# Attention with a soft mixture of experts behind it: the first query block's maxima as an F32 product, and one tile for two heads' last scores

## The chip, the cores and the metric

The kernel runs on one core of a Trainium2 chip. The metric is device time in microseconds (us). Six names recur: PE is TensorE (matmul), PEld its weight loads, DVE is VectorE, ACT is ScalarE, POOL is GpSimd, SP issues the DMAs. PSUM is the memory into which PE writes; SBUF is the main on-chip memory.

## The reference

Eight batches of eight heads attend over 576 tokens of 64 channels, with a decay and a causal mask; then 4608 tokens of 512 channels go through a soft mixture of eight experts with four slots each.

```
scores = q @ k.T / 8 + cum[:, None] - cum[None, :]      # cum = cumsum(log(clip(f)))
scores = where(causal, -1e9, scores); scores -= max(scores, -1)
attn = exp(scores) / (sum(exp(scores)) + 1e-9); x = attn @ v
logits = x @ phi
slots = softmax(logits over tokens).T @ x               # then per expert: relu(s @ w1) @ w2
out = softmax(logits over slots) @ slot_out
```

## The kernel before

Heads are taken in 32 pairs, one pair per turn of the main loop (`for g in range(1, NG)`, L695), four pairs to a batch. `w = (g - 4) % 4` tells which of a batch's side jobs a turn carries: logits at w 0, their maximum and weights at w 1, combine weights and dispatch at w 2 and 3. The order of every engine's work is the order of the calls in the program; an engine takes its instructions in that order, and semaphores make one wait for another. All DMAs are issued by SP in one queue.

For a head there are two passes over the scores. The first finds each query's maximum: `s1` (L215) multiplies a block of 128 queries by the keys that come before it, into one of three PSUM buffers `s`, and `tops` (L230) adds the mask and takes the maximum on DVE (L239: a custom operation and an accumulator read that writes a column of `MT`). `TOPS` lists six such pieces: number 2 is block 4 against keys 0 to 287, where the mask is zero throughout; number 5 is block 0, 64 queries padded to 128 against 64 keys. `mturn` (L244) turns `MT` of a pair on PE, `mrows` copies the rows on ACT, and a DMA puts them into the operand `YA`, so that the second pass gets scores with the maximum already taken off.

The second pass, `s2` (L263), multiplies keys by queries into a ring of three PSUM tiles, as two matmuls for high and low parts (L276, L277). `SEGS` lists the pieces; the last tile of a head holds 256, 192 and 64 columns for key chunks 0, 3 and 4 (piece 5 is chunk 4, 64 keys by 64 queries). `expo` (L283) takes the exponential on ACT into `PTS`, which holds two heads; `causal` (L285) zeroes the triangles on POOL in three operations (L291 for chunks 0 to 2 in one, L294 for chunk 3 and for chunk 4). `s3` (L303) multiplies by the values into `pv[0]` (first head) or `pv[1]` (second head), 25 products a head in the order `VALUES` (L69, L70): products of 64 queries alternate between the lower and the upper 64 partitions of the output (u = 0 and u = 1), 13 of the one kind and 12 of the other. Each F32 product is two matmul instructions. `norm` (L318) divides on DVE.

A turn works on different pairs at once. It does `s2` and `s3` of pair g (heads h0, h1), and `s1` and `tops` of heads u0 = h0 + 3 and u1 = h0 + 4, so that u0 completes the maxima of pair g + 1. The turn starts with `s2(h0, 0)` and `norm` of the head before; `tops(u0)` follows; `mturn(g + 1)` stands after `s2(h1, 2)`; `s3(h0)` and `s3(h1)` end the turn. On DVE `mgroup` (w 1) and `combine(b, 0)` (w 2) stand between `norm` and `tops(u0, 2)`. `px` (L352) turns results of pair g - 1 on PE into free columns of the `pv` tiles, and `xcopy` copies them on ACT; `px(g - 1, 4)` uses columns 325 to 452 of `pv[1]`.

Of the kernel before, what the change touches and what calls it, by code (L numbers as in the profile page):

```python
# [7 lines left out]
F32 = mybir.dt.float32  # L8
# [13 lines left out]
NBLK = 5  # L22
# [45 lines left out]

HALF = [[(t, u, c) for t in (4, 3, 2, 1, 0) if t < 4 or u == 0 for c in range(queries(t, u) // 2 + 1)] for u in range(2)]  # L69
VALUES = [x for n in range(13) for h in HALF for x in h[n : n + 1]]  # L70

@with_exitstack
def attn_softmoe(ctx: ExitStack, tc: tile.TileContext, qk, v, f, phi, w1, w2, cst, out):
# [156 lines left out]
    def tops(i, *which):  # L230
        if not head(i):
            return
        g, h = divmod(i, 2)
        for n in which:
            bank, o, blk, j0, w = TOPS[n]
            t = st["top", i % 2, bank]
            m0 = max(448 - (128 * blk + 64) + j0, 0)
            top = MT[g % 3][:, NBLK * h + blk : NBLK * h + blk + 1] if g else m2[h][:, blk, 1:2]
            nc.vector.tensor_tensor_reduce(  # L239
                out=t[:, o : o + w], in0=t[:, o : o + w], in1=mask[:, m0 : m0 + w], scale=1.0, scalar=top if n == 3 else -3.0e38,  # L240
                op0=ALU.add, op1=ALU.max, accum_out=top,
            )
# [19 lines left out]

    def s2(i, *which):  # L263
        if not head(i):
# [3 lines left out]
        for n in which:  # L268
            bank, c, i0, w = SEGS[n]
            t, at = (turn(), 0) if n < 4 else st["bank"]  # L270

            n = 128 if c < 4 else 64
            o = t[0:n, at : at + w]
            at += w
            j0 = S * h + 128 * c
            nc.tensor.matmul(o, wa[0:m, j0 : j0 + n], ya[0:m, h, 64 + i0 : 64 + i0 + w], start=True, stop=False)  # L276
            nc.tensor.matmul(o, wb[:, j0 : j0 + n], yb[:, h, i0 : i0 + w], start=False, stop=True)  # L277
            st["bank"] = t, at

# [4 lines left out]

    def causal(i):  # L285

# [4 lines left out]
        nc.gpsimd.affine_select(d3, d3, pattern=[[0, 3], [1, 128]], compare_op=ALU.is_ge, fill=0.0, base=0, channel_multiplier=-1)  # L291
        for o, w in ((pt_col(3, 384), 128), (pt_col(4, 512), 64)):
            dd = pt[:, o : o + w]
            nc.gpsimd.affine_select(dd, dd, pattern=[[1, w]], compare_op=ALU.is_ge, fill=0.0, base=0, channel_multiplier=-1)  # L294

    def blank(t):
# [6 lines left out]
    def s3(i, n0=None, n1=None):  # L303
# [4 lines left out]
        for t, u, c in VALUES[n0:n1]:  # L308
# [3 lines left out]
                o[64 * u : 64 * u + 64, t, :], PT[i % 2][:, at : at + 64], V[:, g % 2, c, 65 * h : 65 * h + 65], start=(c == 0), stop=(c == r // 2)  # L312
            )

    def xtile(b, u):
# [188 lines left out]
    load_qk(1)  # L504
    nc.vector.memset(fin, 1.0)
    nc.scalar.activation(fin[:, 0:1], fin[:, 0:1], AF.Ln)
    nc.vector.memset(fy, 1.0)
# [69 lines left out]
    def first(i, n, busy=0):  # L577
        s1(i, *GROUPS[n])
        warm(busy, cs)
        tops(i, *GROUPS[n])  # L580

# [34 lines left out]
    first(2, 3)  # L616
    causal(0)
    low_k(2)
# [19 lines left out]
    low_k(3)  # L638
    causal(1)
    low_q(3)  # L640
# [54 lines left out]
    for g in range(1, NG):  # L695
# [11 lines left out]
        expo(h0, 0)  # L707
        norm(h0 - 1)
        if w == 1:
            mgroup(b)  # L710
# [7 lines left out]
        tops(u0, 3)  # L718
        if g > 1:
            px(g - 1, 0)  # L720
        s2(h0, 2)
        expo(h0, 2)
        if g > 1:
            px(g - 1, 3)
        else:
            round_k(3, 0)
            round_q(3, 0)
# [9 lines left out]
        s2(h0, 4)  # L737
        s1(u0, 4, 5)
        s2(h0, 5)
        expo(h0, 3)  # L740
        tops(u0, 4, 5)
        causal(h0)
# [25 lines left out]
        s2(h1, 3, 4)  # L768
        s1(u1, 4, 5)
        s2(h1, 5)  # L770
        expo(h1, 3)
        tops(u1, 4, 5)
        causal(h1)
# [308 lines left out]
```

## Time and profile before

| | us |
|---|---|
| median of 3 runs | 400.83 (400.12 to 402.21) |
| the profiled execution | 401.76 |
| its span, first to last instruction | 400.1 |
| PE busy | 380.7 (95%) |
| weight loads busy | 333.1 (83%) |
| DVE busy | 282.9 (71%) |
| ACT busy | 262.5 (66%) |
| POOL busy | 250.8 (63%) |

A row of a timeline gives start and duration in us, engine, line, operation, output and inputs, shapes and count; what stands in brackets is the idle time before it and what ended it. Rows of the same kind that follow each other are merged. A weight load has a row of its own (PEld). A matmul's duration contains its way through the array, so the distance from one start to the next is what it costs. Operations of DVE can overlap in the rows: the next starts before the one before has ended. The mean granted clock of TensorE was 0.983.

### The profile page before, as it was taken

Reading aid. Unit: us, or ns where it says so; the run is one execution under the profiler, and the core shown is the slowest. Engines: PE = TensorE matmul, PEld = TensorE weight load, DVE = VectorE, ACT = ScalarE, POOL = GpSimd, SP = SyncE. Lnnn points to the kernel's source line nnn. Section 1 sums busy time; section 2 is a strip of 40 time slices with the busy share of each in tenths; the row PEclk is TensorE's granted clock in tenths of the full one; section 3 lists DMA queues with packets and bytes.
Section 4 is the critical chain, followed back from the end, with each engine's and each line's share of the span. In section 5 each row is a group of like instructions: output and inputs, shape, how many; then the busy total and the mean of one; then the engine's idle time right before and its main releaser. Section 6 shows DMA issues by size and latency. Waiting matters only on the chain.

```text
span 400.1 us, 15146 instructions
## 1 busy us (share of the span) xinstructions
PE 380.7 (95%) x5843; PEld 333.1 (83%) x5843; DVE 282.9 (71%) x1130; ACT 262.5 (66%) x675; POOL 250.8 (63%) x341
## 2 busy tenths in 40 slices
PE   8999999999999999999999999999999998999880
PEld 7889999999989999999999989999999885444540
DVE  7878887879767978787888778877878444312571
ACT  8859777767776777668777786777776542240450
POOL 4697887878767877787878777877787520000000
PEclk9999999999999999999999999999999999999985
DMA  6866767777777777777777677877675699999798
GB/s 206 209 159 161 231 169 207 205 210 209 206 208 207 209 207 208 210 208 207 209 208 225 201 209 204 225 209 214 199 185 151 240 343 350 409 407 387 247 378 333
DMA packets 34744, 93.72 MB, mean 234 GB/s; under 512 B 4282, under 2 KB 9072, under 8 KB 34672
## 3 DMA queue, kind: packets, MB, share of 16 engines
q1 hardware_dynamic: 34672, 92.75, 75.1%
q8 instruction: 46, 0.75, 0.8%
q14 instruction: 26, 0.21, 0.2%
HBM read 63.93 MB, written 9.73 MB: 184 GB/s over the span
## 4 chain that ended last, share of the span: by engine, by line
PE 90%; DMA 3%; ACT 2%; DVE 1%; issue 1%; SPq 0%; DVEq 0%; ACTq 0%
PE pv L311 25%; PE ring L276 13%; PE s L226 12%; PE ring L277 12%; PE pv L338 4%; PE pv L936 4%; PE more L899 4%; PE lg L374 3%; PE ring L491 3%; PE ring L1016 2%; PE ds L455 2%; DMA RAW<-in_qk 2%; DMA out<-RAW 1%; PE ring L684 1%; PE pv L249 1%; ACT PTS L283 1%
## 5 line engine op out<-in xcount | busy, mean ns | idle before, releaser
L283 ACT ACTIVATE PTS<-ring 128x320 f32<-128x320 f32 (+2 forms) x256 | 119.5, 513 | 61.3 <-PE ring L277 33.8
L239 DVE CUSTOM_DVE_ANT_0 s<-s,mask 128x320 f32<-128x320 f32 (+4 forms) x320 | 137.4, 449 | 5.3 <-PE s L226 0.8
L276 PE MATMUL ring<-YA,WA 67*128 67x320 f32 (+9 forms) x384 | 121.8, 330 | 0.0
L277 PE MATMUL ring<-YB,WB 128*128 128x320 f32 (+4 forms) x384 | 110.7, 296 | 0.0
L311 PE MATMUL pv<-V,PTS 128*64 128x65 f32 x3200 | 104.3, 223 | 0.7 <-ACT mr L258 0.7
L311 PEld LDWEIGHTS pv<-V,PTS 128*64 128x64 f32 x3200 | 99.6, 137 | 3.4 <-ACT mr L258 1.2
L226 PE MATMUL s<-WA,YA 66*128 66x288 f32 (+9 forms) x384 | 98.6, 312 | 1.7 <-ACT PTS L283 1.3
L205 POOL TENSOR_TENSOR WB<-RAW,WB 64x576 fp32r<-64x576 f32 x64 | 90.3, 1410 | 11.0 <-DMA WB<-WA 5.0
L210 POOL TENSOR_TENSOR YB<-RAW,YA 64x576 fp32r<-64x576 f32 x64 | 89.3, 1414 | 2.5
L276 PEld LDWEIGHTS ring<-YA,WA 67*128 67x128 f32 (+3 forms) x384 | 69.7, 183 | 5.4 <-issue 2.1
L277 PEld LDWEIGHTS ring<-YB,WB 128*128 128x128 f32 (+1 forms) x384 | 69.9, 182 | 0.0
L226 PEld LDWEIGHTS s<-WA,YA 66*128 66x128 f32 (+1 forms) x384 | 63.0, 190 | 7.8 <-ACT PTS L283 2.4
L294 POOL TENSOR_SCALAR_AFFINE_SELECT PTS<-PTS 128x128 f32<-128x128 f32 (+1 forms) x128 | 31.3, 265 | 35.2 <-ACT PTS L283 32.3
L239 DVE DVE_READ_ACCUMULATOR2_ANT MT<- 128x1 f32 x372 | 52.5, 141 | 0.0
L291 POOL TENSOR_SCALAR_AFFINE_SELECT PTS<-PTS 128x384 f32<-128x384 f32 x64 | 33.3, 520 | 25.8 <-ACT PTS L283 22.8
L179 ACT CAST WA<-RAW 64x576 fp32r<-64x576 f32 x64 | 40.1, 669 | 12.8 <-DMA RAW<-in_qk 12.3
L338 PE MATMUL pv<-cs,X 128*128 128x128 f32 x155 | 42.1, 277 | 0.2 <-DVE lg L805 0.2
L239 DVE CUSTOM_DVE_ANT_0 s<-s,mask,MT 128x288 f32<-128x288 f32 x62 | 32.6, 526 | 11.2 <-PE s L226 2.2
L184 ACT CAST YA<-RAW 64x576 fp32r<-64x576 f32 x63 | 39.4, 669 | 0.4
L326 DVE TENSOR_SCALAR rl<-pv 128x5 f32<-128x5 f32 x64 | 10.5, 164 | 33.2 <-PE pv L311 32.7
L331 DVE TENSOR_TENSOR X<-pv,rl 128x320 f32<-128x320 f32 (+1 forms) x65 | 31.5, 486 | 2.4 <-DMA YA<-mr 0.3
L362 ACT COPY XT<-pv 128x128 f32<-128x128 f32 (+1 forms) x124 | 28.6, 292 | 0.0
(184 smaller groups left out, 353.5 us busy)
## 6 DMA issues: line engine op xcount, KB each, us to landing
w<-in_w SPq DMA_DIRECT2D x46, 512.0 KB
RAW<-in_qk SPq DMA_DIRECT2D x31, 576.0 KB
V<-in_v SPq DMA_DIRECT2D x32, 325.0 KB
YB<-YA SPq DMA_DIRECT2D x30, 288.0 KB
WB<-WA SPq DMA_DIRECT2D x30, 288.0 KB
p<-in_w SPq DMA_DIRECT2D x7, 512.0 KB
out<-p SPq DMA_DIRECT2D x6, 512.0 KB
out<-RAW SPq DMA_DIRECT2D x9, 256.0 KB
```

Of the source, the lines that this page charges most:

```text
L179: nc.scalar.copy(WA[g % 3][0:64, S * h : S * h + S], RAW[g % 3][64:128, h])
L184: nc.scalar.copy(YA[g % 3][0:64, h, 64:640], RAW[g % 3][0:64, h])
L205: nc.gpsimd.tensor_tensor(t[0:64], RAW[g % 3][64:128, h], t[64:128].bitcast(F32), op=ALU.subtract)
L210: nc.gpsimd.tensor_tensor(YB[g % 2][64:128, h], RAW[g % 3][0:64, h], YA[g % 3][0:64, h, 64:640].bitcast(F32), op=ALU.subtract)
L226: nc.tensor.matmul(t[:, o : o + w], ya[0:m, h, 128 * blk : 128 * blk + 128], wa[0:m, j0 : j0 + w], start=True, stop=True)
L239: nc.vector.tensor_tensor_reduce(out=t[:, o : o + w], in0=t[:, o : o + w], in1=mask[:, m0 : m0 + w], scale=1.0, scalar=top if n == 3 else ...
L276: nc.tensor.matmul(o, wa[0:m, j0 : j0 + n], ya[0:m, h, 64 + i0 : 64 + i0 + w], start=True, stop=False)
L277: nc.tensor.matmul(o, wb[:, j0 : j0 + n], yb[:, h, i0 : i0 + w], start=False, stop=True)
L283: nc.scalar.activation(PT[i % 2][:, SEG_O[bank] : SEG_O[bank] + at], t[:, 0:at], AF.Exp, scale=0.125)
L291: nc.gpsimd.affine_select(d3, d3, pattern=[[0, 3], [1, 128]], compare_op=ALU.is_ge, fill=0.0, base=0, channel_multiplier=-1)
L311: nc.tensor.matmul(o[64 * u : 64 * u + 64, t, :], PT[i % 2][:, at : at + 64], V[:, g % 2, c, 65 * h : 65 * h + 65], start=(c == 0), stop=( ...
L338: nc.tensor.transpose(pm[:, 0:128], x[:, t, 128 * (p % 2) : 128 * (p % 2) + 128], ident)
```

## The change

The maxima of block 0 are no longer a piece of `s1` and `tops` in the main loop. Behind the values of a head, at the end of `s3`, stands an F32 product of 64 queries by 64 keys of the head four later, which writes the upper 64 partitions of `pv[1]` in columns 384 to 447 or 448 to 511. `edges`, after `norm` of the next turn, adds the triangle of the mask for both heads in one DVE operation and takes both maxima in a second one, on partitions 64 to 127, into `MT`. Heads 0 to 4 keep the old way. Piece 2 is taken with a plain reduction, without the mask, in all heads.

Chunk 4 of the second pass leaves the last tile of both heads. `corners` computes it for both heads into a ring tile of its own, after `expo(h1, 3)`, with one exponential and one POOL operation for the two, which stands before `causal(h1)`. `causal` in the loop has two operations then. Query block 4, which alone reads chunk 4, moves from the head of `VALUES` to its end. `px(g - 1, 0)` moves behind `s2(h0, 2)`. Three small memsets of `MT` on POOL are added at the start.

```diff
@@ -66,7 +66,7 @@
-HALF = [[(t, u, c) for t in (4, 3, 2, 1, 0) if t < 4 or u == 0 for c in range(queries(t, u) // 2 + 1)] for u in range(2)]
+HALF = [[(t, u, c) for t in (3, 2, 1, 0, 4) if t < 4 or u == 0 for c in range(queries(t, u) // 2 + 1)] for u in range(2)]
 VALUES = [x for n in range(13) for h in HALF for x in h[n : n + 1]]
 @with_exitstack
@@ -236,6 +236,9 @@
             t = st["top", i % 2, bank]
             m0 = max(448 - (128 * blk + 64) + j0, 0)
             top = MT[g % 3][:, NBLK * h + blk : NBLK * h + blk + 1] if g else m2[h][:, blk, 1:2]
+            if n == 2:
+                nc.vector.tensor_reduce(top, t[:, o : o + w], axis=AX.X, op=ALU.max)
+                continue
             nc.vector.tensor_tensor_reduce(
                 out=t[:, o : o + w], in0=t[:, o : o + w], in1=mask[:, m0 : m0 + w], scale=1.0, scalar=top if n == 3 else -3.0e38,
                 op0=ALU.add, op1=ALU.max, accum_out=top,
@@ -260,14 +263,17 @@
         dst = YA[g % 3][m : m + 1, h0:h1].rearrange("c h s -> c (h s)")
         nc.sync.dma_start(dst.bitcast(F32), mr[0:n].bitcast(F32))
-    def s2(i, *which):
+    def s2(i, *which, corner=None):
         if not head(i):
             return
         g, h = divmod(i, 2)
         ya, wa, yb, wb, m = YA[g % 3], WA[g % 3], YB[g % 2], WB[g % 2], TOP[g % 3] + 1
         for n in which:
             bank, c, i0, w = SEGS[n]
-            t, at = (turn(), 0) if n < 4 else st["bank"]
+            if corner is None:
+                t, at = (turn(), 0) if n < 4 else st["bank"]
+            else:
+                t, at = corner, 64 * h
             n = 128 if c < 4 else 64
             o = t[0:n, at : at + w]
@@ -275,23 +281,36 @@
             j0 = S * h + 128 * c
             nc.tensor.matmul(o, wa[0:m, j0 : j0 + n], ya[0:m, h, 64 + i0 : 64 + i0 + w], start=True, stop=False)
             nc.tensor.matmul(o, wb[:, j0 : j0 + n], yb[:, h, i0 : i0 + w], start=False, stop=True)
-            st["bank"] = t, at
+            if corner is None:
+                st["bank"] = t, at
     def expo(i, bank):
         if head(i):
             t, at = st["bank"]
             nc.scalar.activation(PT[i % 2][:, SEG_O[bank] : SEG_O[bank] + at], t[:, 0:at], AF.Exp, scale=0.125)
-    def causal(i):
+    def corners(g):
+
+        t = turn()
+        for h in range(2):
+            s2(2 * g + h, 5, corner=t)
+        o = pt_col(4, 512)
+        to = PTS[:, 0:3200].rearrange("p (h c) -> p h c", h=2)[0:64, :, o : o + 64]
+        nc.scalar.activation(to, t[0:64, 0:128].rearrange("p (h c) -> p h c", h=2), AF.Exp, scale=0.125)
+        nc.gpsimd.affine_select(to, to, pattern=[[0, 2], [1, 64]], compare_op=ALU.is_ge, fill=0.0, base=0, channel_multiplier=-1)
+
+    def causal(i, *more):
         if not head(i):
             return
         pt = PT[i % 2]
         d3 = pt[:, 0:960].rearrange("p (a b) -> p a b", b=320)[:, :, 0:128]
         nc.gpsimd.affine_select(d3, d3, pattern=[[0, 3], [1, 128]], compare_op=ALU.is_ge, fill=0.0, base=0, channel_multiplier=-1)
-        for o, w in ((pt_col(3, 384), 128), (pt_col(4, 512), 64)):
+        for o, w in ((pt_col(3, 384), 128), *more):
             dd = pt[:, o : o + w]
             nc.gpsimd.affine_select(dd, dd, pattern=[[1, w]], compare_op=ALU.is_ge, fill=0.0, base=0, channel_multiplier=-1)
+
+    LAST = (pt_col(4, 512), 64)
     def blank(t):
@@ -311,6 +330,19 @@
             nc.tensor.matmul(
                 o[64 * u : 64 * u + 64, t, :], PT[i % 2][:, at : at + 64], V[:, g % 2, c, 65 * h : 65 * h + 65], start=(c == 0), stop=(c == r // 2)
             )
+        if n1 is None and i and head(i + 4):
+
+            ya, wa, m = YA[(g + 2) % 3], WA[(g + 2) % 3], TOP[(g + 2) % 3]
+            nc.tensor.matmul(
+                pv[1][64:128, 384 + 64 * h : 448 + 64 * h], ya[0:m, h, 64:128].bitcast(F32), wa[0:m, S * h : S * h + 64].bitcast(F32), start=True, stop=True
+            )
+
+    def edges(g, h0=0):
+        if pair(g):
+            t = pv[1][64:128, 384:512].rearrange("p (h c) -> p h c", h=2)[:, h0:2]
+            tri = mask[64:128, 384:448].rearrange("p (o c) -> p o c", o=1).broadcast_to([64, 2 - h0, 64])
+            nc.vector.tensor_tensor(t, t, tri, op=ALU.add)
+            nc.vector.tensor_reduce(MT[g % 3][64:128, NBLK * h0 : 2 * NBLK : NBLK], t, axis=AX.X, op=ALU.max)
     def xtile(b, u):
         return X[(2 * b + u) % 3 if (b, u) != (B - 1, 1) else 3]
@@ -503,6 +535,8 @@
     nc.sync.dma_start(cs, cst[:, 0:258])
     load_qk(1)
     nc.vector.memset(fin, 1.0)
+    for t in MT:
+        nc.gpsimd.memset(t, 0.0)
     nc.scalar.activation(fin[:, 0:1], fin[:, 0:1], AF.Ln)
     nc.vector.memset(fy, 1.0)
     for t in ring:
@@ -575,9 +609,10 @@
     GROUPS = ((0, 1), (2,), (3,), (4, 5))
     def first(i, n, busy=0):
-        s1(i, *GROUPS[n])
+        ns = GROUPS[n]
+        s1(i, *ns)
         warm(busy, cs)
-        tops(i, *GROUPS[n])
+        tops(i, *ns)
     def both(i, n):
         s2(i, *((0,), (1,), (2,), (3, 4, 5))[n])
@@ -614,7 +649,7 @@
     load_qk(3)
     first(2, 2)
     first(2, 3)
-    causal(0)
+    causal(0, LAST)
     low_k(2)
     low_q(2)
     both(1, 0)
@@ -636,7 +671,7 @@
     first(3, 3)
     norm(0)
     low_k(3)
-    causal(1)
+    causal(1, LAST)
     low_q(3)
     first(4, 0)
     warm(2, cs)
@@ -706,6 +741,7 @@
         s2(h0, 0)
         expo(h0, 0)
         norm(h0 - 1)
+        edges(g + 1, int(g == 1))
         if w == 1:
             mgroup(b)
         if w == 2:
@@ -716,11 +752,10 @@
         expo(h0, 1)
         s1(u0, 3)
         tops(u0, 3)
-        if g > 1:
-            px(g - 1, 0)
         s2(h0, 2)
         expo(h0, 2)
         if g > 1:
+            px(g - 1, 0)
             px(g - 1, 3)
         else:
             round_k(3, 0)
@@ -735,10 +770,9 @@
             xcopy(g - 1, (3,))
             px(g - 1, 2)
         s2(h0, 4)
-        s1(u0, 4, 5)
-        s2(h0, 5)
+        s1(u0, 4)
         expo(h0, 3)
-        tops(u0, 4, 5)
+        tops(u0, 4)
         causal(h0)
         low_k(h0 + 2)
         if w == 1:
@@ -766,10 +800,10 @@
         s1(u1, 0, 1)
         tops(u1, 0, 1)
         s2(h1, 3, 4)
-        s1(u1, 4, 5)
-        s2(h1, 5)
+        s1(u1, 4)
         expo(h1, 3)
-        tops(u1, 4, 5)
+        corners(g)
+        tops(u1, 4)
         causal(h1)
         low_k(h1 + 2)
         if g == 1:
```

## Rows read from the trace of the kernel before

**Rows 1.** The page's first part (engine, busy us, share, instructions) and the head of its fourth (the chain that ended last, by engine).
```profile
PE 380.7 (95%) x5843; PEld 333.1 (83%) x5843; DVE 282.9 (71%) x1130; ACT 262.5 (66%) x675; POOL 250.8 (63%) x341
...
PE 90%; DMA 3%; ACT 2%; DVE 1%; issue 1%; SPq 0%; DVEq 0%; ACTq 0%
```

**Rows 2.** The waits of PE, longest in total first (us in total, times, longest): the first two.
```profile
PE ring L491 <- DVE ring L510: 1.9, 1, 1.9
PE s L226 <- ACT PTS L283: 1.3, 2, 0.8
```

**Rows 3.** The timeline of PE in a turn with w 3 (g = 19), from 204.7 to the start of the next turn.
```profile
204.72 0.41 PE L226 MATMUL s<-WA,YA 66*128 66x448 f32 x2
204.97 0.22 PE L276 MATMUL ring<-YA,WA 67*64 67x64 f32 x1
205.03 0.22 PE L277 MATMUL ring<-YB,WB 128*64 128x64 f32 x1
205.09 0.45 PE L276 MATMUL ring<-YA,WA 67*128 67x448 f32 x1
205.37 0.37 PE L277 MATMUL ring<-YB,WB 128*128 128x448 f32 x1
205.58 0.27 PE L338 MATMUL pv<-cs,X 128*128 128x128 f32 x1
...
206.57 0.27 PE L249 MATMUL pv<-cs,MT 128*10 128x128 f32 x1
...
207.39 0.42 PE L226 MATMUL s<-WA,YA 97*128 97x448 f32 x2
207.65 0.22 PE L276 MATMUL ring<-YA,WA 67*64 67x64 f32 x1
207.71 0.22 PE L277 MATMUL ring<-YB,WB 128*64 128x64 f32 x1
207.86 3.25 PE L311 MATMUL pv<-V,PTS 128*64 128x65 f32 x100
211.04 0.47 PE L276 MATMUL ring<-YA,WA 67*128 67x448 f32 x1
```

**Rows 4.** The timeline of DVE in the same turn, from the norm of the head before to the last maximum of u0.
```profile
202.27 0.17 DVE L326 TENSOR_SCALAR rl<-pv 128x5 f32<-128x5 f32 x1 [0.53 <-PE pv L311]
...
202.69 0.49 DVE L331 TENSOR_TENSOR X<-pv,rl 128x320 f32<-128x320 f32 x1
203.10 0.46 DVE L239 CUSTOM_DVE_ANT_0 s<-s,mask 128x288 f32<-128x288 f32 x1
203.47 0.14 DVE L239 DVE_READ_ACCUMULATOR2_ANT MT<- 128x1 f32 x1
203.76 0.53 DVE L239 CUSTOM_DVE_ANT_0 s<-s,mask,MT 128x288 f32<-128x288 f32 x1
...
205.72 0.14 DVE L239 DVE_READ_ACCUMULATOR2_ANT MT<- 128x1 f32 x1
205.90 0.23 DVE L239 CUSTOM_DVE_ANT_0 s<-s,mask 128x64 f32<-128x64 f32 x1
206.05 0.14 DVE L239 DVE_READ_ACCUMULATOR2_ANT MT<- 128x1 f32 x1
```

**Rows 5.** The timeline of all engines in the turn before (w 2, g = 18), where the last maximum of u0 and the turning of `MT` meet.
```profile
196.26 0.14 DVE L239 DVE_READ_ACCUMULATOR2_ANT MT<- 128x1 f32 x1
...
196.46 0.09 PEld L249 LDWEIGHTS pv<-cs,MT 128*10 128x10 f32 x1 [0.17 <-DVE MT L239]
196.46 0.28 PE L249 MATMUL pv<-cs,MT 128*10 128x128 f32 x1
```

**Rows 6.** Groups of DVE instructions by line and form (count, busy us, mean ns, idle before).
```profile
L483 DVE TENSOR_REDUCE ring<-ring 128x5 f32<-128x160 f32 x8 | 2.6, 327 | 4.4 <-ACT ring L479 4.4
L486 DVE TENSOR_TENSOR ctok<-ring,sm 128x160 f32<-128x160 f32 x8 | 2.6, 325 | 0.3
L389 DVE TENSOR_REDUCE mb<-LG 128x1 f32<-128x193 f32 x7 | 2.5, 355 | 6.8 <-ACT LG L381 6.8
L475 DVE TENSOR_REDUCE sm<-tk 128x5 f32<-128x160 f32 x7 | 2.3, 326 | 3.2 <-ACT LD L444 3.2
L239 DVE CUSTOM_DVE_ANT_0 s<-s,mask 128x64 f32<-128x64 f32 x64 | 14.9, 232 | 2.2
```

**Rows 7.** The timeline of DVE at the start of the program: memsets of all partitions (L526), then of partitions 64 to 127 (L299, L300).
```profile
4.45 0.08 DVE L526 MEMSET LG<- 128x10 f32 x2
4.54 0.11 DVE L299 MEMSET pv<- 64x64 f32 x1
4.73 0.06 DVE L300 MEMSET pv<- 64x1 f32 x1
4.75 0.11 DVE L299 MEMSET pv<- 64x64 f32 x1
```

**Rows 8.** The timeline of DVE near the end: a copy that starts at partition 0, then a subtraction that starts at partition 64 (L1003).
```profile
376.52 0.42 DVE L1017 COPY p<-ring 128x256 f32<-128x256 f32 x1 [0.91 <-PE ring L1016]
376.98 0.43 DVE L1003 TENSOR_TENSOR SO<-more,SO 64x256 fp32r<-64x256 f32 x1
```

**Rows 9.** All waits: those of two DVE lines of the side jobs, and of the weight load of `mturn` (us in total, times, longest).
```profile
DVE mb L389 <- ACT LG L381: 6.8, 7, 1.2
...
DVE sm L475 <- ACT LD L444: 3.2, 5, 1.5
...
PEld pv L249 <- DVE MT L239: 1.1, 6, 0.2
```

**Rows 10.** The timeline of all engines in the turn with w 3: the exponential of the second head's last tile and POOL's operations on that head.
```profile
208.05 0.60 ACT L283 ACTIVATE PTS<-ring 128x512 f32<-128x512 f32 x1 [0.52 <-POOL WB L205]
208.09 0.52 POOL L291 TENSOR_SCALAR_AFFINE_SELECT PTS<-PTS 128x384 f32<-128x384 f32 x1
...
208.71 0.49 POOL L294 TENSOR_SCALAR_AFFINE_SELECT PTS<-PTS 128x128 f32<-128x128 f32 x2
```

## The prediction

> **What bounds the kernel now.** I read the page's busy shares and its chain first, then PE's waits, then the timelines of one turn. PE is busy 95% of the span and carries 90% of the chain that ended last [rows 1]; after the start its longest wait adds up to 1.3 us in all [rows 2]. So the main loop runs at the rate of PE's instructions. In a turn with w 3 PE goes without a gap from 202.2 to 211.04, and the last 3.2 us of it are the values, 100 matmuls two at a time [rows 3].
>
> That is not the whole picture. DVE has a chain through the same turn that begins and ends on PE: the values of the head before end, `norm` begins at 202.27 and from there DVE works on with no idle time that matters until the last maximum of u0 is read at 206.05 + 0.14 = 206.19 [rows 4]; `mturn` on PE needs that maximum and starts at 206.57 [rows 3], 0.38 later. How small can the 0.38 get? In the turn with w 2 the weight load is released by DVE: the read ends at 196.26 + 0.14 = 196.40 and the transpose starts at 196.46 [rows 5]. So 0.06 is the least, and the DVE chain has 0.32 us in hand in turns with w 0 and w 3. In six turns it is already late, by 0.2 at most [rows 9]. From `mturn` on, PE must still do the second half of the turn. The change has to be judged on both: what it takes from PE, and what it does to these 0.32 us.
>
> **The change, part by part.** *PE, first half.* From the 448-column product of u0 to the next turned block 204.72 to 205.58 = 0.86 us pass; in it stand the product that goes (64 columns) and the two of chunk 4 that move [rows 3]. A 448-column matmul whose weights are already in takes 205.58 - 205.37 = 0.21. Without the small ones, in whose shadow no weight load of 128 columns can hide, I take three times 0.21 = 0.63: 0.23 less. Of this only 205.03 - 204.97 and its like (some 0.1) are sure; the rest is my choice, since rows with two long matmuls behind each other show 0.21. The moved `px` issues the same transposes; I put it at nothing, 0.05 either way.
>
> *PE, second half.* Before: 207.39 to 207.86 = 0.47, with the small product and two of chunk 4. After: 0.21 for the long one, four of chunk 4 at 0.06 for three steps (205.03 - 204.97, 205.09 - 205.03), and 0.15 from the last to the values (207.86 - 207.71): 0.54, so 0.07 more [rows 3].
>
> *The F32 product.* Two instructions a head behind 50. A head has 26 instructions for the lower 64 partitions and 24 for the upper, and 3.18 us for 100 is 26 pairs of places per head of 0.06 each [rows 3]; the last product is alone in its two places, and the new one writes the other half. I take 0. The other bound is two places of its own, 0.12 a head (a rival below).
>
> *DVE, `edges`.* Two operations on partitions 64 to 127. The nearest rows are 160 elements: 0.325 for the addition, 0.327 for the reduction [rows 6]. At the slope between 64 and 448 columns in the maxima (0.23 to 0.63, 0.001 a column [rows 4]) 128 elements make 0.29 each; bounds are 0.23 and 0.36 [rows 6]. The question is what lies between. Operations that start at the same partition overlap: `norm`'s product starts at 202.69, takes 0.49, and the next starts after 0.41 [rows 4]; the second memset at partition 64 starts before the one ahead of it has ended (4.75 against 4.73 + 0.06). From partition 0 to partition 64 nothing overlaps: 4.54 against 4.53, though no wait is shown [rows 7], and the subtraction on the upper half starts at 376.98, 0.04 after the end of the copy [rows 8]. The Trainium skill says so as a rule (VectorE: DVE Perf Modes, section "Two Vector instructions with no wait between them"): an instruction whose input or output begins in another group of 32 partitions than the last one's starts only when all before it have finished; the trace agrees. `edges` crosses twice. So from `norm`'s product to the next maximum: 0.49 + 0.04 + 0.29 + 0.03 (the reduction depends on the addition, as 202.47 on 202.44) + 0.29 + 0.04 = 1.18 instead of 0.41: 0.77 more. With overlap at both crossings it would be some 0.23 less.
>
> *DVE, what goes.* Piece 2 as a plain reduction of 288: 0.46 by the same slope (below by 0.36 for 193 elements, above by 0.53), no accumulator read; the next piece still waits for two engines, which costs the 0.15 from 203.61 to 203.76, so 0.61 against 0.66 (203.10 to 203.76): 0.05 less. Piece 5: the end moves from 206.19 to 205.72 + 0.14 = 205.86, 0.33 less [rows 4]. Together DVE's chain becomes 0.77 - 0.05 - 0.33 = 0.39 longer. Behind `edges` all of u0's maxima are queued, and behind them `mturn` and all of PE.
>
> *Turns with w 0 and 3, and g 2 and 3 (15).* `mturn` comes at 0.39 - 0.32 = 0.07 later; PE would be there 0.23 earlier and waits 0.3. Then 0.07 for the second half: 0.14 a turn, +2.1.
>
> *Turns with w 1 (7).* DVE waits there for ACT's copy of the logits, 6.8 us in 7 times, 0.97 each [rows 9]; `edges` (0.69 from the end of `norm`) is hidden in it. The chain becomes 0.38 shorter, PE stays the bound: -0.23 + 0.07 = -0.16, -1.1. Without this cover a turn costs 0.14 like the others.
>
> *Turns with w 2 (7).* DVE waits for ACT in 5 of them, 3.2 us, 1.5 the longest [rows 9], so some 0.44 in each of four. Two without cover: 0.69 - 0.38 + 0.07 = +0.38 each; four: 0.69 - 0.44 - 0.38 + 0.07 = -0.06 each; one: -0.23. Together +0.3.
>
> *ACT and POOL.* The last tile is 64 columns shorter and one exponential of 128 columns a pair is new; POOL does three operations a head pair less one. The new wait: POOL's triangle for chunk 4 stands before the second head's two, and behind these `low_k`. By my clock the last corner matmul starts 0.07 + 0.21 + 0.18 after 207.39, at 207.85; from such a start (207.71) to the exponential 0.34 pass [rows 3, 10], which gives 208.19; 0.3 for it, 0.1 to POOL, 0.25, then 0.52 and 0.29: the second head's triangles are ready at 209.4 and 209.7. Its values start at 207.86 + 0.14 + 1.59 = 209.6 and reach the first diagonal chunk four products (0.23) on, and chunk 3 seven products (0.41) on: 209.8 and 210.0. Free, with 0.3 to spare. No DMA is added or moved in SP's queue. The memsets at the start lie beside the first loads.
>
> **Sum.** +2.1 - 1.1 + 0.3 = +1.3. The profiled execution took 401.76 (span 400.1), which becomes 403.1; it was 0.9 above the median of 400.83, and against that I predict **402.1**.
>
> **Rivals.**
> *B. PE's gain comes through.* If DVE overlaps at the crossings or `edges` is cheaper by 0.23, `mturn` comes 0.16 earlier and a turn of the 15 takes 0.09 less: -1.4; w 1 -1.1; w 2 -0.23 in five turns and +0.15 in two. 397.5. For it: only five rows show crossings, none of them in PSUM between reads like these. Against it: they all show the same.
> *C. The product has places of its own.* If the two last products of a head do not pair, the first head's 0.12 goes into the 15 turns and both heads' into the 14 others: 1.8 + 3.3 on top, 407; with one place (0.06) 404.7. It decides from the first place that is not shared. For it: in-order issue, both instructions of one product standing behind each other. Against: 100 matmuls in 3.18 us already run two at a time.
> *D. Small matmuls cost only their columns.* The 64-column product is followed after 204.97 - 204.72 - 0.21 = 0.04; if that is all PE gets back, w 1 turns lose 0.03 instead of gaining 0.16: 403.4. The Trainium skill leans to this (TensorE: Matmul & The Clock Gate, section "Back-to-back issue gap"): columns by 2.4 GHz and 2.5 ns, an estimate of 0.03 us for 64, which the rows agree with for this one step. Against it: the 0.29 between the two long matmuls behind chunk 4 (205.09 to 205.37) where 0.21 would do.
>
> **How the numbers follow.** My forecast has 0.50 (own range 400.6 to 403.6, from 0.06 a turn in `edges` and the reduction), B 0.27, C 0.13, D 0.10. About 0.5%, 2.0 us, is what a measurement can tell from no change, so the bounds are 398.8 and 402.8. The forecast gives 0.01 faster, 0.33 same, 0.16 slower; B 0.23 and 0.04 same; C 0.01 same and 0.12 slower; D 0.02 and 0.08. Together 0.24, 0.40, 0.36. The range reaches to B's centre and to C's nearer case: 397.0 to 405.0.
>
> **What would show it.** In the profile after: the weight load of `mturn` waits for DVE in most turns with w 0 and 3, 0.2 to 0.4 us each (right) or hardly ever (B). Between `norm` and the first maximum 1.1 to 1.2 us (right) or 0.95 (overlap). The values of a pair take 3.2 us (right) or 3.3 to 3.4 (C). From the long product to the turned block 0.63 in the first half (right) or 0.8 (D). The prediction is wrong if PE waits for POOL at the second head's values, or if turns with w 0 and 3 are shorter than before.

## The result and the profile after

The changed kernel takes **403.96 us** (403.58 to 404.94), the kernel before 400.88 (400.12 to 402.21): ratio 1.0075, 95% interval 1.0059 to 1.0091. It is slower by 3.1 us, where the prediction had 402.1 and a range of 397.0 to 405.0. The profiled execution took 403.62, its span is 401.9.

The page of the changed kernel: engines (busy us, share, instructions), and the chain that ended last.
```profile
PE 380.2 (95%) x5902; PEld 326.8 (81%) x5902; DVE 281.2 (70%) x1008; ACT 269.9 (67%) x706; POOL 244.9 (61%) x313
...
PE 80%; DVE 13%; DMA 2%; issue 2%; ACT 1%; DVEq 0%; SPq 0%
```
The busy times move by 3% at most against [rows 1]. The chain moves more: DVE has 13% of it where it had 1%. PE has as much to do as before, but a part of its time now hangs on DVE, and the waits say where (us in total, times, longest).
```profile
PEld s L226 <- DVE MT L242: 4.9, 15, 0.3
...
PEld s L226 <- ACT PTS L290: 4.5, 7, 0.6
...
PE s L226 <- DVE ctok L508: 2.6, 6, 0.4
...
PEld pv L252 <- DVE MT L242: 1.3, 8, 0.3
```
In the 15 turns with w 0 and 3 and g 2 and 3 PE waits 0.3 for a buffer `s` that DVE has not yet read (L226 is `s1`), and in seven of them then 0.15 for the maxima at `mturn` (L252). The other two rows are turns with w 2.

DVE in the turn with w 3 (g = 19), which answers to [rows 4]:
```profile
203.78 0.49 DVE L363 TENSOR_TENSOR X<-pv,rl 128x320 f32<-128x320 f32 x1
204.30 0.31 DVE L344 TENSOR_TENSOR pv<-pv,mask 64x128 f32<-64x128 f32 x1
204.64 0.30 DVE L345 TENSOR_REDUCE MT<-pv 64x2 f32<-64x128 f32 x1
204.97 0.46 DVE L240 TENSOR_REDUCE MT<-s 128x1 f32<-128x288 f32 x1
205.57 0.53 DVE L242 CUSTOM_DVE_ANT_0 s<-s,mask,MT 128x288 f32<-128x288 f32 x1
...
207.51 0.14 DVE L242 DVE_READ_ACCUMULATOR2_ANT MT<- 128x1 f32 x1
```
From `norm`'s product to the first maximum 1.19 pass instead of 0.41, and the last read of u0 ends at 207.65, 3.87 after that product, instead of 3.50 before (206.19 - 202.69).

PE in the same turn, which answers to [rows 3]:
```profile
205.72 0.38 PE L226 MATMUL s<-WA,YA 66*128 66x448 f32 x1
...
206.35 0.27 PE L370 MATMUL pv<-cs,X 128*128 128x128 f32 x1
...
207.12 0.40 PE L226 MATMUL s<-WA,YA 97*128 97x288 f32 x1
...
207.71 0.28 PE L252 MATMUL pv<-cs,MT 128*10 128x128 f32 x1
...
209.06 1.67 PE L330 MATMUL pv<-V,PTS 128*64 128x65 f32 x49
210.52 0.22 PE L336 MATMUL pv<-WA,YA 97*64 97x64 f32 x1
...
212.25 0.47 PE L282 MATMUL ring<-YA,WA 67*128 67x448 f32 x1
```
From the long product to the turned block 0.63, as forecast; then 0.3 of waiting before 207.12, and `mturn` 0.06 behind DVE's last read. A turn, measured from one first product of scores (L282, 448 columns) to the next, lasts in microseconds (worked out from PE's timelines; w 2 is g = 6, undisturbed in the kernel before):

| kernel | w 3, g 19 | w 1, g 17 | w 2, g 6 | median |
|---|---|---|---|---|
| before | 8.88 | 9.43 | 10.05 | 400.88 |
| after | 9.04 | 9.35 | 10.54 | 403.96 |
| all 128 partitions | 8.89 | 9.35 | 10.39 | 401.01 |
| sum in SBUF, 64 partitions | 9.00 | 9.33 | 10.50 | 403.23 |
| sum in SBUF, 128 partitions | 8.75 | 9.35 | 10.33 | 398.65 |
| without the product | 8.83 | 9.41 | 10.07 | 399.12 |
| without the corner tile | 8.91 | 9.32 | 10.58 | 402.29 |
| product in `pv[0]`, earlier | 8.69 | 9.36 | 9.99 | 396.02 |

Over the loop of the two profiled executions the 15 turns with w 0 and 3 and g 2 and 3 cost 2.2 us more, those with w 1 0.9 less, those with w 2 0.6 more: 1.9 in all. Beside this the medians differ by 3.1, to which I come back.

### The profile page after: what moved, and what is told of

Read it like the earlier page. It is cut to its first block, busy times and chain, and to the rows that moved or that the text cites. A ratio compares the mean times of both kernels' runs of the same rounds, so it can differ in the third digit from the quotient of the medians.

```text
span 401.9 us, 15128 instructions
## 1 busy us (share of the span) xinstructions
PE 380.2 (95%) x5902; PEld 326.8 (81%) x5902; DVE 281.2 (70%) x1008; ACT 269.9 (67%) x706; POOL 244.9 (61%) x313
## 4 chain that ended last, share of the span: by engine, by line
PE 80%; DVE 13%; DMA 2%; issue 2%; ACT 1%; DVEq 0%; SPq 0%
PE pv L330 25%; PE ring L282 11%; PE s L226 10%; PE ring L283 10%; DVE s L242 5%; PE pv L970 4%; PE more L933 4%; PE lg L406 3%; PE pv L370 3%; PE ring L1050 2%; PE ds L487 2%; DVE MT L240 2%; DMA out<-RAW 1%; PE pv L252 1%; PE ring L719 1%
## 5 line engine op out<-in xcount | busy, mean ns | idle before, releaser
L290 ACT ACTIVATE PTS<-ring 128x448 f32<-128x448 f32 (+1 forms) x256 | 119.9, 496 | 53.2 <-PE ring L283 39.9
L282 PE MATMUL ring<-YA,WA 67*128 67x320 f32 (+9 forms) x384 | 116.5, 317 | 0.0
L283 PE MATMUL ring<-YB,WB 128*128 128x320 f32 (+4 forms) x384 | 107.6, 296 | 0.0
L226 PE MATMUL s<-WA,YA 97*128 97x320 f32 (+5 forms) x325 | 98.3, 338 | 4.6 <-DVE ctok L508 2.6
L242 DVE CUSTOM_DVE_ANT_0 s<-s,mask 128x320 f32<-128x320 f32 (+2 forms) x197 | 95.4, 510 | 3.3 <-PE s L226 0.9
L282 PEld LDWEIGHTS ring<-YA,WA 67*128 67x128 f32 (+3 forms) x384 | 69.6, 181 | 5.3 <-issue 2.1
L226 PEld LDWEIGHTS s<-WA,YA 66*128 66x128 f32 (+1 forms) x325 | 56.4, 190 | 14.5 <-DVE MT L242 4.9
L370 PE MATMUL pv<-cs,X 128*128 128x128 f32 x155 | 36.5, 272 | 0.0
L242 DVE DVE_READ_ACCUMULATOR2_ANT MT<- 128x1 f32 x251 | 35.6, 142 | 0.0
L311 POOL TENSOR_SCALAR_AFFINE_SELECT PTS<-PTS 128x128 f32<-128x128 f32 x66 | 18.9, 288 | 21.7 <-ACT PTS L290 20.9
L240 DVE TENSOR_REDUCE MT<-s 128x1 f32<-128x288 f32 x62 | 28.1, 454 | 0.7
```

Of the source, the lines that this page charges most:

```text
L226: nc.tensor.matmul(t[:, o : o + w], ya[0:m, h, 128 * blk : 128 * blk + 128], wa[0:m, j0 : j0 + w], start=True, stop=True)
L240: nc.vector.tensor_reduce(top, t[:, o : o + w], axis=AX.X, op=ALU.max)
L242: nc.vector.tensor_tensor_reduce(out=t[:, o : o + w], in0=t[:, o : o + w], in1=mask[:, m0 : m0 + w], scale=1.0, scalar=top if n == 3 else ...
L290: nc.scalar.activation(PT[i % 2][:, SEG_O[bank] : SEG_O[bank] + at], t[:, 0:at], AF.Exp, scale=0.125)
L370: nc.tensor.transpose(pm[:, 0:128], x[:, t, 128 * (p % 2) : 128 * (p % 2) + 128], ident)
```

## The experiments

All ratios are against runs of the kernel before on the same chip (400.8 to 401.3 there).

**Both DVE operations on all partitions.**
```diff
-            t = pv[1][64:128, 384:512].rearrange("p (h c) -> p h c", h=2)[:, h0:2]
+            t = pv[1][:, 384:512].rearrange("p (h c) -> p h c", h=2)[:, h0:2]
...
-            nc.vector.tensor_reduce(MT[g % 3][64:128, NBLK * h0 : 2 * NBLK : NBLK], t, axis=AX.X, op=ALU.max)
+            nc.vector.tensor_reduce(MT[g % 3][:, NBLK * h0 : 2 * NBLK : NBLK], t, axis=AX.X, op=ALU.max)
```
The mask is taken with all its rows too, and the lower half of those columns, which stands for no query of block 0, is set to zero once.

> The two operations of edges run on all 128 partitions instead of 64 to 127; the rows added hold nothing that is used. Theory T (the loss is DVE's chain from norm to mturn, made 0.4 us longer by edges, of which 0.23 us are the two changes of the start partition, where nothing overlaps): the step from norm's product to the first maximum falls from 1.19 us to about 0.95, turns with w 0 and 3 go back to 0.0 to 0.1 us under before, and the time is 399.0 to 401.0 us (after: 403.96). Rival R3 (the changes of partition cost nothing, the two operations are what they are): 403.5 to 404.5. Rival R1 (the loss is the corner tile: its exponential, its POOL operation and the second half of PE's turn): 403.5 to 404.5.

401.01 (400.57 to 402.04), ratio 1.0001, 0.9992 to 1.001: level with the kernel before. So the choice of 64 partitions alone cost 3 us. But look at which of the two changes of partition went away. DVE in that kernel, turn g = 19:
```profile
202.10 0.49 DVE L363 TENSOR_TENSOR X<-pv,rl 128x320 f32<-128x320 f32 x1
202.63 0.30 DVE L344 TENSOR_TENSOR pv<-pv,mask 128x128 f32<-128x128 f32 x1
202.96 0.29 DVE L345 TENSOR_REDUCE MT<-pv 128x2 f32<-128x128 f32 x1
203.17 0.45 DVE L240 TENSOR_REDUCE MT<-s 128x1 f32<-128x288 f32 x1
```
Behind the reduction the next maximum starts 0.21 on, before it has ended (0.33 after the change): 0.12 back. But the addition still starts 0.53 after `norm`'s product, though both start at partition 0. Something besides the partition holds it; two runs at the end of this section tell what.

**Without the product.** The main loop takes block 0 by `s1` and `tops` again; the corner tile, the plain reduction of piece 2 and the order of the values stay.
```diff
-        edges(g + 1, int(g == 1))
...
-        s1(u0, 4)
+        s1(u0, 4, 5)
...
-        tops(u0, 4)
+        tops(u0, 4, 5)
...
```

> Block 0's maxima are taken as before (a piece of s1 and tops), no F32 product and no edges; the corner tile, the plain reduction for piece 2, the order of px and of the values stay as changed. T: the wait of mturn for DVE is gone from turns with w 0 and 3, these are within 0.1 us of before, and the time is 400.0 to 401.5 us. R1: at least 403.

399.12 (398.6 to 399.41), ratio 0.9947, 0.9934 to 0.9959. I had not expected this kernel to beat the one before: the rest of the change is a gain of 1.8 us, and the product with `edges` costs nearly 5 on top of it.

**Without the corner tile.** `edges` stays, chunk 4 goes back into the last tile of each head.
```diff
         s1(u0, 4)
+        s2(h0, 5)
         expo(h0, 3)
         tops(u0, 4)
-        causal(h0)
+        causal(h0, LAST)
...
-        corners(g)
...
```

> The corner tile is undone (chunk 4 again in each head's last tile, its own POOL operation), block 0's product and edges stay. T: the DVE chain stays as long as after the change, only the 0.07 us of PE's second half come back in each turn that DVE bounds: 401.5 to 403.0 us. R1: back to before, 400.5 to 401.3.

402.29 (401.94 to 402.66), ratio 1.0031, 1.002 to 1.0042, in the theory's range. With `edges` in place the corner tile is a loss of 1.7 us; without `edges` it is a gain together with the order of the values and the moved `px` (below), and no run has the tile alone there. The turns with w 0 and 3 show why: with and without it `mturn` starts 4.50 after the start of the turn, since DVE sets that; what the tile saves on PE in the first half goes into the wait. From there to the values pass 1.35 with the tile and 1.24 without, so the two small products that it brings into the second half, at 0.06 each, are paid in full. In turns with w 2 `mturn` does come sooner with the tile, at 4.77 for 4.94, and the tile pays for itself there (10.54 for 10.58).

**What the rest is worth.** Two more runs: the plain reduction of piece 2 alone in the kernel before, and the run without the product with piece 2 masked and accumulated as before.
```diff
+            if n == 2:
+                nc.vector.tensor_reduce(top, t[:, o : o + w], axis=AX.X, op=ALU.max)
+                continue
```

> The kernel before with one edit alone: piece 2 of the maxima is a plain reduction. Theory T: PE bounds the turns and DVE has 0.3 us in hand, so the 0.05 to 0.2 us saved on DVE a head buys nothing: 400.5 to 401.2. Rival R: the gain of the run without the product (399.12) comes from here, since piece 2's buffer is handed back to PE sooner: 399.0 to 399.9.

400.52, ratio 0.9985, 0.997 to 1.0: at most a little.

> The run without the product, but piece 2 as before, masked and accumulated: what is left of the change is the last key chunk of both heads in one tile and the order of the values. Theory T: the gain of the run without the product comes from this part, on PE and ACT: 399.0 to 399.8. Rival R: it comes from the plain reduction: 400.5 to 401.2. If both parts give some of it, between, and the two differences from the kernel before add up to 1.8 within 0.5.

399.89, ratio 0.9966, 0.995 to 0.9983. In per cent the corner tile with the order of the values gives 0.34 and the plain reduction 0.15, both together 0.53 (by medians 0.92 and 0.29 us, together 1.85): each may give a share, the intervals do not settle it closer.

**The kernel before, profiled again.**

> The kernel before, unchanged, profiled in another execution. Disputed are three stretches of the first profile in which PE waits for ACT and PTS (turns g 9, 10 and 22, some 1.7 us together), which the profile of the changed kernel and that of the run without the product do not have. Theory T: they are accidents of one execution; this profile has them elsewhere or not at all, the other turns with w 2 last 10.05 within 0.1, and the turns with w 0 and 3 agree with the first profile within 0.03. Rival R: they belong to the order of the kernel before; the same three turns are long again, by the same amounts within 0.1.

401.57. Of the 22 undisputed turns with w 0, 1 or 3 or at the start only one moved by more than 0.03 (g = 13, +0.20). Turn 9 is 9.43 there, as its like; but turns 10, 14, 18, 22 and 26 are again over 10.2 (10.75, 11.15, 10.24, 10.26, 10.24 after 11.12, 10.39, 10.25, 10.82, 10.39). Neither side was right: with w 2 the lateness stands in the same five turns, with another size each time, and with w 1 it moved from turn 9 to turn 13. With w 2 it is DVE's combination that waits for ACT, 3.2 us in the first profile [rows 9] and 2.7 in this one; in the changed kernel that wait is gone. Above clean turns it comes to 3.1 us in the first profile and 2.6 in this one; in the changed kernel no such turn is late. Its longest waits in the two profiles are alike, 1.3 [rows 2] and, here, the same two times:
```profile
PE s L226 <- ACT PTS L283: 1.2, 2, 0.8
```

**The order in turns with w 2.** The combination ahead of `edges`, in those turns alone.
```diff
-        edges(g + 1, int(g == 1))
+        if w != 2:
+            edges(g + 1, int(g == 1))
...
         if w == 2:
             combine(b, 0)
+            edges(g + 1)
```

> The changed kernel, in turns with w 2 alone the combination stands ahead of the two operations of the F32 product; nothing is left out. Theory T: u0's maxima and the transpose behind them wait for both, in whichever order, so those turns stay at 10.54 within 0.1 and the time at 403.5 to 404.5. Rival R: PE loses 0.4 a turn in waiting for the buffer that the combination reads; it comes free some 0.7 sooner, turns with w 2 last 10.0 to 10.25, time 400.8 to 402.3.

405.16, ratio 1.0101, 1.0077 to 1.0126. Turn 6 lasts 10.50, as the theory said (the time lies 0.7 above its range). The rows show PE's wait gone and nothing gained. The changed kernel, w 2, g = 18:
```profile
194.85 0.48 PE L226 MATMUL s<-WA,YA 66*128 66x320 f32 x2 [0.43 <-DVE ctok L508]
...
197.44 0.27 PE L252 MATMUL pv<-cs,MT 128*10 128x128 f32 x1
```
With the order turned round, the same place:
```profile
194.17 0.48 PE L226 MATMUL s<-WA,YA 66*128 66x320 f32 x2
...
197.39 0.28 PE L252 MATMUL pv<-cs,MT 128*10 128x128 f32 x1
```
PE comes to these scores 0.68 earlier, and `mturn` moves by 0.05. The last maximum's read of u0, in the changed kernel and then here:
```profile
197.15 0.14 DVE L242 DVE_READ_ACCUMULATOR2_ANT MT<- 128x1 f32 x1
...
197.19 0.14 DVE L242 DVE_READ_ACCUMULATOR2_ANT MT<- 128x1 f32 x1
```
It ends at 197.29, 0.15 before `mturn`, and here at 197.33, 0.06 before it. So the wait with a name and 2.6 us beside it could give back 0.09 at most: the maxima stood right behind it. Why the time lies above the range stays open; two of these turns are late in this profile (10.69 and 11.13 at g = 10 and 26).

**The place of the product.** First both heads' products behind the first head's values, in the same tile `pv[1]`, and `edges` behind the first head's `norm`, where DVE otherwise waits.
```diff
-        if n1 is None and i and head(i + 4):
+        if n1 is None and i and head(i + 4) and (i == 1 or h == 0):
...
+            for k in (1,) if i == 1 else range(2):
...
-        edges(g + 1, int(g == 1))
...
         s3(h0)
         norm(h0)
+        edges(g + 2)
```

> Both products of a pair stand behind the values of the first head, one turn ahead of mturn, and edges follows norm of the first head on DVE, where DVE otherwise waits for PE; so edges leaves the chain from norm of the second head to mturn. T: mturn no longer waits for DVE, turns with w 0 and 3 become 0.05 to 0.15 us shorter than before, w 2 about as before, and the time is 398.5 to 400.5 us, under both kernels. R1: 403 or more, since the corner tile is the same. A rival to both (C, products need places of their own on PE): the values of a pair take 3.2 us or more from first to last start instead of 3.03, and the time is 401 or more.

451.84, ratio 1.1263: far off. One wait is the whole of it.
```profile
PE pv L330 <- DVE MT L346: 47.2, 28, 1.7
```
The second head's values write other columns of `pv[1]`, yet PE holds them until DVE's reduction of the product has ended. Then `edges` left as in the changed kernel, but moved behind the maxima of pieces 0 and 1:
```diff
-        edges(g + 1, int(g == 1))
...
         tops(u0, 0, 1)
+        edges(g + 1, int(g == 1))
```

> The changed kernel with the two operations of the F32 product moved behind the maxima of pieces 0 and 1 of u0; nothing is left out. Theory T: the length of DVE's chain up to the transpose of the maxima is what counts, and it is the same length: turns with w 0, 2 and 3 stay as after within 0.06, time 403.4 to 404.4, though PE's waits for the buffers of the scores (4.9 us for DVE MT at the scores' line) shrink to under 2 and the transpose waits longer instead. Rival R: the turns with w 2 are lost on the buffer that the combination reads behind these two operations; they go back to some 10.1 to 10.3, and the time to 401.0 to 402.6.

511.36, ratio 1.2709; missed the same way.
```profile
PE pv L370 <- DVE MT L345: 53.7, 30, 2.0
```
This time it is `px`, which turns a block into `pv[1]` right behind. So in this program the tile, not the column, is what PE waits for, and the question of the place becomes one of the tile. The third run is the first of these with the products, and `edges`, in `pv[0]`.
```diff
-                    pv[1][64:128, 384 + 64 * k : 448 + 64 * k], ya[0:m, k, 64:128].bitcast(F32), wa[0:m, S * k : S * k + 64].bitcast(F32), start=True, stop=True
+                    pv[0 if i > 1 else 1][64:128, 384 + 64 * k : 448 + 64 * k], ya[0:m, k, 64:128].bitcast(F32), wa[0:m, S * k : S * k + 64].bitcast(F32), start=True, stop=True
...
-            t = pv[1][64:128, 384:512].rearrange("p (h c) -> p h c", h=2)[:, h0:2]
+            t = pv[at][64:128, 384:512].rearrange("p (h c) -> p h c", h=2)[:, h0:2]
...
```

> Nothing is left out. Both heads' F32 products of pair g+2 stand behind the first head's values as in the early run, but in the first values tile (pv 0, upper 64 partitions, columns 384 to 512), which PE next writes in the following turn; the two DVE operations stand behind the first head's norm, where DVE otherwise waits for the second head's values. Theory T: the operations cost only by their place ahead of u0's maxima. Taken out of it, DVE's chain to the transpose is some 0.38 shorter than in the kernel before, PE bounds the turns and keeps what the product and the corner tile save it: turns with w 0 and 3 get 0.10 to 0.20 shorter than before, those with w 2 go back to 9.9 to 10.4; 396.0 to 398.5, below the run without the product (399.12). Rival R1: the two products take places of their own on PE between the heads' values, 0.12 to 0.25 a turn, and eat the gain: 399.0 to 402. Rival R2: the first values tile collides too (transposes of the outputs, of the maxima, logits), and PE waits for DVE: over 405.

**396.02** (395.67 to 396.49), ratio 0.9867, 0.9847 to 0.9886: faster than both kernels, 5.3 us below the runs of the kernel before beside it, with nothing left out. DVE at the end of turn g = 19 and on into the next:
```profile
206.34 0.49 DVE L364 TENSOR_TENSOR X<-pv,rl 128x320 f32<-128x320 f32 x1
206.86 0.31 DVE L345 TENSOR_TENSOR pv<-pv,mask 64x128 f32<-64x128 f32 x1
207.21 0.30 DVE L346 TENSOR_REDUCE MT<-pv 64x2 f32<-64x128 f32 x1
...
207.96 0.49 DVE L364 TENSOR_TENSOR X<-pv,rl 128x320 f32<-128x320 f32 x1
208.37 0.45 DVE L240 TENSOR_REDUCE MT<-s 128x1 f32<-128x288 f32 x1
```
The two operations are no shorter, and the addition is still held (0.52 behind `norm`'s product), but they stand behind the first head's `norm`, and behind the second head's `norm` the first maximum is back at 0.41. DVE's share of the chain falls to 1%:
```profile
PE 89%; ACT 3%; DMA 3%; DVE 1%; issue 1%; SPq 0%; DVEq 0%
```

**What holds the addition.** The sum goes to a small SBUF tile instead of back into `pv`, once with 64 and once with all partitions.
```diff
-            nc.vector.tensor_tensor(t, t, tri, op=ALU.add)
+            ed = small.tile([P, 2, 64], F32, name=f"ed{g}", tag="ed", bufs=1)[64:128, h0:2]
+            nc.vector.tensor_tensor(ed, t, tri, op=ALU.add)
...
```

> The changed kernel, but the addition of the mask writes its sum to a small tile in SBUF instead of back into the values tile that norm's product reads, and the reduction reads it there; upper 64 partitions as in the changed kernel, nothing left out. Disputed: why the addition starts 0.52 after norm's product starts (203.78 to 204.30), where maxima start after 0.41. Theory T: either cause is enough, the change of start partition or the write to the tile that is still being read; here the change of partition is left, so still 0.50 to 0.54, and 403.3 to 404.5. Rival R: the change of partition does nothing at this place, the written tile alone does: 0.40 to 0.43, turns with w 0, 2 and 3 some 0.1 shorter, 401.5 to 402.6.

403.23 (402.83 to 404.12), ratio 1.0051, 1.0035 to 1.0068: 0.07 below the theory's range, and above the rival's.
```profile
203.24 0.49 DVE L364 TENSOR_TENSOR X<-pv,rl 128x320 f32<-128x320 f32 x1
203.76 0.29 DVE L345 TENSOR_TENSOR ed<-pv,mask 64x128 f32<-64x128 f32 x1
204.09 0.28 DVE L346 TENSOR_REDUCE MT<-ed 64x2 f32<-64x128 f32 x1
204.41 0.46 DVE L240 TENSOR_REDUCE MT<-s 128x1 f32<-128x288 f32 x1
```

> The run with both operations on all 128 partitions (401.01), with its sum in a small SBUF tile as well; nothing left out. Neither a change of start partition nor a written tile is left between norm's product and the addition. Theory T: the addition starts 0.40 to 0.43 after norm's product instead of 0.53 (202.10 to 202.63), turns with w 0 and 3 get some 0.1 shorter, 399.3 to 400.4. Rival R: something else holds the addition (the operands in PSUM, or the kind of operation); 0.50 to 0.54 and 400.6 to 401.6 as without the edit.

398.65 (397.74 to 398.95), ratio 0.9931, 0.9915 to 0.9947, somewhat below the theory's range.
```profile
201.00 0.49 DVE L364 TENSOR_TENSOR X<-pv,rl 128x320 f32<-128x320 f32 x1
201.41 0.28 DVE L345 TENSOR_TENSOR ed<-pv,mask 128x128 f32<-128x128 f32 x1
201.72 0.29 DVE L346 TENSOR_REDUCE MT<-ed 128x2 f32<-128x128 f32 x1
201.93 0.45 DVE L240 TENSOR_REDUCE MT<-s 128x1 f32<-128x288 f32 x1
```
With the partition changed and the sum elsewhere the addition starts after 0.52, with the same partition and the sum in place after 0.53, with neither after 0.41. Either cause is enough by itself. From `norm`'s product to the first maximum the four kernels have 1.19, 1.07, 1.17 and 0.93 (after; all partitions; SBUF with 64; SBUF with 128), and the turns with w 3 follow: 9.04, 8.89, 9.00, 8.75. Whether it is the chip that holds the write to a tile still being read or a wait in the program, no run here tells.

## Why the prediction was right or wrong, point by point

*DVE's chain: right.* `edges` was put at 1.18 from `norm`'s product to the next maximum and took 1.19; the single terms were 0.01 to 0.02 too small for the operations (0.31 and 0.30 for 0.29). The chain became 3.87 - 3.50 = 0.37 longer (forecast 0.39), and `mturn` comes 0.09 later in a turn (4.50 for 4.41; forecast 0.07).

*Its reason, "two changes of start partition" at 0.23: right in size, incomplete in cause.* The pair of SBUF runs gives 1.17 - 0.93 = 0.24. But in this kernel the first one would have been paid anyway, since the sum is written to the tile that `norm` reads: all partitions give back 0.12, not 0.23. The rule of the Trainium skill that the prediction named (VectorE: DVE Perf Modes, section "Two Vector instructions with no wait between them") agrees with the second crossing, 0.33 against 0.21, and with the SBUF pair, 0.52 against 0.41. By it alone the addition on all partitions would not be held, which its 0.53 contradicts unless something else made it wait. Rival B (overlap at the crossings) falls: nothing overlapped.

*PE's first half, -0.23: right for w 0 and 3.* 0.63 from the long product to the turned block (205.72 to 206.35). Rival D, which gave the small matmuls only their columns, falls. *Second half, +0.07: right*, 1.35 from `mturn` to the values against 1.29.

*The product at nothing: right.* The values last 3.03 from the first to the last start in both kernels; the row at 210.52 stands among pairs. Rival C falls; in the best run, too, the products cost 0.01 at most (3.04).

*Turns with w 0 and 3: right.* +0.14 forecast; 0.15 measured (0.16 at g = 19), 2.2 us for 2.1. Where PE waits was only half right: most of it falls on a buffer `s` (4.9 us) and not on `mturn`, which is the same chain seen one buffer earlier.

*Turns with w 1: size off.* Forecast -0.16 each, -1.1; an undisturbed one gained 0.08. The cover held: DVE's wait for ACT fell from 6.8 us to 1.5. But the 0.23 had been read in a turn with w 3. In one with w 1 a turning of `mb` on PE stays between the long products, and from the long product to the turned block it went from 0.89 to 0.73, 0.16 less (g = 17, before and after):
```profile
184.98 0.41 PE L226 MATMUL s<-WA,YA 97*128 97x448 f32 x2
...
185.87 0.27 PE L338 MATMUL pv<-cs,X 128*128 128x128 f32 x1
...
185.84 0.38 PE L226 MATMUL s<-WA,YA 97*128 97x448 f32 x1
186.06 0.27 PE L428 MATMUL pv<-cs,mb 128*1 128x128 f32 x1
...
186.57 0.27 PE L370 MATMUL pv<-cs,X 128*128 128x128 f32 x1
```
`mturn` came 0.15 sooner (4.38 to 4.23), and of that 0.09 was left at the start of the values. The 0.9 in the profile contains 0.36 from turn 9, which was late before.

*Turns with w 2: the step that failed, in its size.* For a turn without cover I took +0.38; turn 6 measured +0.49. `edges` itself was right, 0.71 for 0.69: the combination starts 1.20 behind `norm`'s product (192.82 to 194.02), and in the undisturbed turn before the change 0.49 (74.25 to 74.74). The rest lies at `mturn`, which comes 0.41 later in the turn (4.77 for 4.36; forecast 0.31): `norm`'s product starts 0.03 later, and PE, held for the combination's buffer until 194.85, comes to `mturn` 0.15 behind DVE's last read, where it was 0.09. DVE in turn g = 18 after the change:
```profile
192.82 0.49 DVE L363 TENSOR_TENSOR X<-pv,rl 128x320 f32<-128x320 f32 x1
193.35 0.31 DVE L344 TENSOR_TENSOR pv<-pv,mask 64x128 f32<-64x128 f32 x1
193.69 0.30 DVE L345 TENSOR_REDUCE MT<-pv 64x2 f32<-64x128 f32 x1
194.02 0.33 DVE L507 TENSOR_REDUCE sm<-tk 128x5 f32<-128x160 f32 x1
```
DVE in turn g = 6 before it:
```profile
74.25 0.49 DVE L331 TENSOR_TENSOR X<-pv,rl 128x320 f32<-128x320 f32 x1
74.74 0.33 DVE L475 TENSOR_REDUCE sm<-tk 128x5 f32<-128x160 f32 x1
```
The waits for ACT did act as cover in these two profiles: the five turns of 10.25 to 11.12 all last 10.52 to 10.54 after the change. But I counted them at one size, and it differs from execution to execution, as the second profile showed. Against undisturbed turns the change costs 15 times 0.15, less 7 times 0.08, and 6 times 0.49 and 0.38 (g = 30): 5.0 us. The profile of before held 3.1 us of late turns which the changed kernel does not have; 5.0 - 3.1 is the 1.9 that the two profiles differ by. So the loss hides in lateness that was there anyway, and how much it shows depends on the execution.

*From the profile to the median.* I carried the offset of the profiled execution over, 0.9 above the median. The one after lies 0.34 below its median (403.62 against 403.96), and these two offsets, 0.88 and 0.34, are the 1.2 between 1.9 in the profiles and 3.1 in the medians. That an execution of the kernel before with less lateness is simply a faster one would explain it; only profiled executions have rows, so this is argued and not shown. So the sum of +1.3 fell short of the profiles by 0.6, most of it in w 1 and w 2, and by 1.2 more in the step to the median. The chain that I named is the one that costs, but its sum is too small: 403.96 lies above the forecast's own range (400.6 to 403.6), and inside the whole range only because that reached up to the nearer case of rival C, which fell. That much is luck.

*ACT and POOL: right.* No wait of PE for POOL appears; POOL ends chunk 3's triangle at 210.60, 7.39 after the start of the turn at 203.21 (forecast 209.7 in a turn from 202.16, so 7.54).

## What to carry to other kernels

Ask of an added operation less what it costs than what is queued behind it: the same two DVE operations lost 3.1 us ahead of the maxima that PE needs, and the whole change gained 5.3 when they stood where DVE was idle. Before moving such work, look up who writes next to the tile that it reads, since PE waited for the tile and not for the columns. And a saving on one engine ahead of a point that another engine sets is worth nothing, while its cost behind that point is paid in full, as the corner tile showed beside `edges`.

## What was not expected of the hardware

A write to the tile that the operation before still reads kept DVE from overlapping as a change of start partition does: 0.53 and 0.52 against 0.41 between starts, be it by the chip or by a wait in the program.

PE's clock. In the run with `edges` behind the maxima PE waits 54 us, but it is 107 us slower than the changed kernel. PE is busy 60 us longer there (440.3 for 380.2) with the same 5902 instructions. The mean granted clock is 0.856, and the stretches of one turn (us, PE busy with matmuls in brackets, granted clock, DMA share, GB/s) show the rest:
```profile
204.90:206.90 2.00, 0.00 (x0) 1.00 0.97 377
206.90:207.90 1.00, 0.99 (x8) 0.99 0.08 32
207.90:212.00 4.10, 4.10 (x18) 0.50 0.00 0
```
PE stood still for 2.0, went on at full clock for 1.0, and then had 0.50, its lower level of 1.2 GHz, while it was busy without a gap. In the early run, with 28 waits of up to 1.7, the mean stayed at 0.989.
